# First DFT stage of batches 1 to 7 on quarters of the PE array, four rows at a time

## The chip, the cores and the metric

The kernel runs on one core of one Trainium2 chip. The metric is the device time of one execution in microseconds (us); lower is better. Three runs of the kernel before took 2705.15, 2701.14 and 2705.21 us, median 2705.15.

## The reference

A global filter over the sequence (real FFT along 3008 positions, multiply by a learned complex filter, inverse FFT) and then a feed-forward layer with the activation h - tanh(h), all in float32:

```python
X = np.fft.rfft(x, axis=1)                     # x: 8 x 3008 x 256
Y = X * (filt_r + 1j * filt_i)[None]           # filt: 1505 x 256
y = np.fft.irfft(Y, n=3008, axis=1)
t = y.reshape(24064, 256)
h = t @ w_in                                   # 256 -> 2048
out = (h - np.tanh(h)) @ w_out                 # 2048 -> 256
```

## The kernel before, in words

The transform is done as matmuls. 3008 = 64 x 47, so position n is 47q + r. Sequence rows r and 47 - r are handled together: partitions 0 to 63 of a tile hold the 64 values of q for row r, partitions 64 to 127 those for row 47 - r. So there are 24 such row pairs (r = 0 to 23) for a batch.

- The **first stage** (`first`, L241 to L265) multiplies a row pair by one constant 128x128 matrix `f` (64 + 64 rows in; 4 kinds of 32 frequencies out): one matmul `pf` of 128 rows, 128 columns out and 256 moving columns for each r. XH = 2 values of r make one step: two matmuls into one PSUM bank (L262), a copy by ScalarE to SBUF (`a1`, L263), and a store to a DRAM buffer `ct1` (L264). Each step loads its own piece of `f` (128 KB) and of x. This covers batches 2 to 7 whole and the last two thirds of batch 1: 80 steps. Batch 0 and the rest of batch 1 go through other code in the prologue.
- The **middle stage** (`middle`, L357) reads `ct1` back, goes across the 24 rows (`forth`: matmuls `pa`, `pb`; VectorE forms sums and differences from PSUM, L306 and L307), multiplies by the filter (`filtered`, its last two instructions are L338 and L339), goes back (`back`: matmuls `pe`) and stores `ct2`.
- The **last stage** (`last`, matmuls `pu`) makes 512 tokens at a time (a group; six groups make a batch). Then the feed-forward layer runs over a group in four **units** (u = 0 to 3, 512 of the 2048 hidden columns each): `up` (matmuls `x`, `y`, `z`, L485), `shrink` (the activation: ScalarE L597, L600, L603; VectorE L607), `down` (matmuls `o`, L655). Both products are done by a Strassen-like scheme with seven products, whose operand sums are made on GpSimd (L465 to L468). The first four units (U = 0 to 3) use plain products (`up_plain` L555, `down_plain` L709) while the weights are still converted from float64.

There are 192 units, U = 0 to 191; batch p's feed-forward is units 24p to 24p + 23. The order on every engine is written out by hand. Inside a unit there are five places, `t(0)` to `t(4)`, at which one step of another stage is put in. For a unit U of 4 or above, outside batch 0, TensorE's order is: X product 1, Y product 2, `t(0)`, four `o` matmuls, `t(1)`, X6, Z5, four `o`, `t(2)`, X7, four `o`, X4, `t(3)`, two `o`, `t(4)`, Z3. VectorE empties Y by L508 (after `t(0)`'s instructions in its own order), X by L533, Z by L525 and L541. `planned(p)` spreads the steps of the first stage of batch p + 2 and of the middle stage of batch p + 1 evenly over batch p's units and sorts them by due position. Batch 2's first stage, with what is left of batch 1, lies closer, in units 0 to 6.

PSUM has eight banks: `x`, `y`, `z` for `up`, `o0` to `o3` for `down`, and one, `t`, for the steps put in. `zd` (L1138) gives a step bank `t`, or at some places bank `y` where the step before it holds `t`: at `t(3)` bank `y` if `t(2)` didn't use it; at `t(4)` and `t(0)` always `t`.

In the prologue, `tiled` (L900) keeps TensorE busy until x has landed. It does so with matmuls on a constant tile in four forms: whole array, quarters (up to 64 rows in, 64 columns out), halves (up to 64 rows, 128 columns), whole array.

Of the kernel before, what the change touches and what calls it, by code (L numbers as in the profile page):

```python
# [9 lines left out]
F32 = mybir.dt.float32  # L10
# [5 lines left out]
ALU = mybir.AluOpType  # L16
# [9 lines left out]
XH = 2  # L26
# [21 lines left out]
def _consts():  # L48
# [9 lines left out]
    f = np.zeros((2, NQ, NH, 4, NA))  # L58
    g = np.zeros((4, NA, NH, 2, NQ))
    for r in range(NH):  # L60
        for half, n in ((0, r), (1, NR - r)):
# [4 lines left out]
            f[half, :, r, 0, :-1], f[half, :, r, 1, :-1] = c, -s  # L66
            f[half, :, r, 2, :-1], f[half, :, r, 3, :-1] = -odd * s, odd * c
            plus, minus = (1 + sign(n)) / 2, (1 - sign(n)) / 2
            f[half, :, r, 0, -1], f[half, :, r, 2, -1] = plus, minus
            f[half, :, r, 1, -1], f[half, :, r, 3, -1] = odd * plus, odd * minus  # L70
# [3 lines left out]
            g[1, -1, r, half], g[3, -1, r, half] = odd * plus, odd * minus  # L74
# [18 lines left out]
    f = f[:, :, :, ORDER, :]  # L93
    return [np.ascontiguousarray(v, dtype=np.float32)
            for v in (f.reshape(128, -1), f[:, :, :, 0:2].reshape(128, -1), g.reshape(128, -1), mats, np.eye(128))]

@with_exitstack
def kernel(
# [11 lines left out]
    f_d, half_d, g_d, mats_d, one_d = (nc.inline_tensor(v, name=n).ap()  # L110
                               for v, n in zip(_consts(), ("f", "f_half", "g", "mats", "one")))
# [6 lines left out]

    filt_d = nc.dram_tensor("filt", (len(SLOTS) * KM, 4, DM), F32, kind="Internal")
# [109 lines left out]
    def load_x(t, b, r, n):  # L229
# [3 lines left out]
        if r == 0:  # L233
            nc.sync.dma_start(t[64:128, 0, :], dram(x.tensor, b * SEQ * DM,
                                                    [[NR * DM, 64], [1, DM]]))
        lo = 1 if r == 0 else 0
        nc.sync.dma_start(t[64:128, lo:n, :], dram(x.tensor, (b * SEQ + NR - r - lo) * DM,
                                                   [[NR * DM, 64], [-DM, n - lo], [1, DM]]))
        return t

    def first(b, z, also=()):  # L241
# [3 lines left out]
        def begin(k):  # L245
            b, c = jobs[k]
            w = XH * 128
            f = tr.tile([128, XH, 128], F32, tag="f", bufs=3, name="f")
            nc.sync.dma_start(f, f_d[:, w * c:w * (c + 1)])
            return load_x(tr.tile([128, XH, DM], F32, tag="x", bufs=3, name="x_sb"),  # L250
# [4 lines left out]
        for k, (b, c) in enumerate(jobs):  # L255
            if k + 2 < len(jobs):
                began.append(begin(k + 2))
            xt, f = began.pop(0)
            pf = z("pf", [128, XH, DM])
            a1 = tr.tile([128, XH, DM], F32, tag="a1", bufs=2, name="a1")  # L260
            for i in range(XH):
                nc.tensor.matmul(pf[:, i], f[:, i], xt[:, i], start=True, stop=True)  # L262
            ACT.copy(a1, pf)  # L263
            ACT.dma_start(dram(ct1[b], XH * c * DM, [[NH * DM, 128], [1, XH * DM]]), a1)  # L264
            yield  # L265
# [145 lines left out]
    def turned_rows():  # L411

        for v, src in enumerate((filt_r.tensor, filt_i.tensor)):
            G.dma_start(dram(filt_d, (turned * 4 + 2 + v) * DM,
                             [[DM // 2, 2], [4 * DM, NH], [1, DM // 2]]),
                        dram(src, SEQ // 2 * DM,
                             [[DM // 2, 2], [-NQ * DM, NH], [1, DM // 2]]))
# [430 lines left out]
    psums = []  # L848

    def z1(name, shape):  # L850
        return psums[-1](name, shape)

    with tc.tile_pool(name="tr", bufs=2) as tr, tc.manual_schedule():
# [12 lines left out]
        with tc.tile_pool(name="pro", bufs=1) as pro, \  # L866
# [32 lines left out]

            def tiled():  # L900

                t = filt[2][:, 0]
                banks = [z0("warm", [128, 256]) for _ in range(4)]

                def mm(rows, cols, bank):
                    nc.tensor.matmul(bank[cols], t[rows, 0:cols.stop - cols.start],
                                     t[rows], start=True, stop=True)

                half = slice(0, 64), slice(64, KM)
                out = slice(0, 64), slice(64, 128)  # L910
                for _ in range(6):
                    mm(slice(0, KM), slice(0, 128), banks[0])
                for n in range(4):
                    for i, rows in enumerate(half):
                        for cols in out:
                            mm(rows, cols, banks[2 * (n % 2) + i])
# [398 lines left out]
```

## Time and profile before

| | |
|---|---|
| runs | 2705.15, 2701.14, 2705.21 us |
| profiled execution: time, span | 2702.15 us, 2700.3 us |
| granted TensorE clock over the span | 0.998 |
| TensorE busy | 2670.9 us, 99% |
| ScalarE, VectorE, GpSimd busy | 1722.8, 1651.3, 1289.9 us |
| first stage (L262): matmul instructions, busy | 320, 82.2 us |

A row of a view names the line of the kernel, the engine, the operation, what it writes and reads, how many, and microseconds. PE is TensorE's matmul, PEld its weight load, DVE VectorE, ACT ScalarE, POOL GpSimd, SP the queue that issues most DMAs. A float32 matmul shows as two instructions, so "x4" is two matmuls. The shape "128*128 128x256" is rows in * columns out of the array, then rows x moving columns.

### The profile page before, as it was taken

The page shows a single profiled execution, that of the slowest core. Times are in us where ns is not written, and L with a number is a line of the kernel's source. Part 1 is how long each engine was busy: PE and PEld are TensorE (multiplying, and loading weights), DVE is VectorE, ACT ScalarE, POOL GpSimd, SP SyncE. Part 2 cuts the span into 40 slices and gives each one's busy share as a digit, 9 for nine tenths or more (in the row PEclk, how much of TensorE's full clock was granted, in tenths as well). Part 3 has the DMA queues.
Part 4 walks back from the last instruction along what each step waited for, and adds up shares of the span by engine and source line. Part 5 has one row for each costly group of instructions (what it writes and reads, how often), then busy time and mean ns, then how long its engine had stood idle before and what let it go on. Part 6 is the DMA issues. An engine that isn't in the chain of part 4 may idle for free.

```text
span 2700.3 us, 36549 instructions
## 1 busy us (share of the span) xinstructions
PE 2670.9 (99%) x12950; PEld 2360.7 (87%) x12950; DVE 1651.3 (61%) x2083; ACT 1722.8 (64%) x2595; POOL 1289.9 (48%) x1082
## 2 busy tenths in 40 slices
PE   8999999999999999999999999999999999999998
PEld 7578889988898888988889888898889988898887
DVE  6777766666566664666546665566655666544545
ACT  3566666666666666666666666666666666666665
POOL 4124555454454445545445554455445554554552
PEclk9999999999999999999999999999999999999999
DMA  8754223431242223323233232323322231110110
GB/s 219 233 162 115 56 58 77 107 86 49 63 110 75 80 56 78 98 69 81 54 96 80 68 86 57 92 76 79 88 55 58 52 79 34 31 40 19 24 24 18
DMA packets 341400, 208.09 MB, mean 77 GB/s; under 512 B 227096, under 2 KB 303492, under 8 KB 341144
## 3 DMA queue, kind: packets, MB, share of 16 engines
q1 hardware_dynamic: 298957, 147.45, 22.6%
q10 hardware_dynamic: 38138, 45.63, 5.5%
q0 software_dynamic: 4112, 12.60, 1.7%
q8 instruction: 104, 1.70, 0.3%
q14 instruction: 89, 0.72, 0.1%
HBM read 133.42 MB, written 74.97 MB: 77 GB/s over the span
## 4 chain that ended last, share of the span: by engine, by line
PE 93%; DMA 2%; DVE 2%; ACT 1%; issue 1%; SPq 1%; ACTq 0%; POOL 0%; DVEq 0%
PE o L655 40%; PE x L485 23%; PE z L485 11%; PE y L485 6%; PE pu L447 3%; PE pe L349 3%; PE pf L262 2%; PE pa L301 2%; PE pb L301 1%; PE o L709 1%; DMA gt<-g 0%; DMA mats_sb<-mats 0%; DMA f<-f 0%; ACT y L597 0%; PE o L555 0%
## 5 line engine op out<-in xcount | busy, mean ns | idle before, releaser
L655 PE MATMUL o<-t,wd 128*128 128x256 f32 (+1 forms) x3008 | 759.7, 375 | 0.0
L607 DVE TENSOR_TENSOR h<-h,y 128x1024 f32<-128x1024 f32 (+1 forms) x384 | 513.3, 1337 | 295.7 <-ACT y L603 295.2
L465 POOL TENSOR_TENSOR t<-h 128x512 f32<-128x512 f32 (+1 forms) x186 | 254.1, 1366 | 907.7 <-DVE h L607 836.1
L655 PEld LDWEIGHTS o<-t,wd 128*128 128x128 f32 x3008 | 570.5, 190 | 67.2
L485 PE MATMUL x<-tu,wu 128*128 128x256 f32 (+1 forms) x2256 | 573.0, 376 | 1.6 <-ACT u L491 1.1
L655 PE MATMUL o<-h,wd 128*128 128x256 f32 (+1 forms) x2256 | 570.4, 375 | 1.8 <-DVE h L607 1.8
L485 PEld LDWEIGHTS x<-tu,wu 128*128 128x128 f32 x2256 | 421.5, 190 | 57.5 <-ACT u L491 9.6
L655 PEld LDWEIGHTS o<-h,wd 128*128 128x128 f32 x2256 | 424.2, 190 | 50.3 <-DVE h L607 2.6
L491 ACT COPY s<-x 128x512 f32<-128x512 f32 (+1 forms) x188 | 108.6, 578 | 501.9 <-PE x L485 483.8
L597 ACT ACTIVATE y<-h 128x1024 f32<-128x1024 f32 (+1 forms) x384 | 400.2, 1042 | 13.3 <-ACT a L263 5.2
L600 ACT ACTIVATE y<-y 128x1024 f32<-128x1024 f32 (+1 forms) x384 | 399.2, 1039 | 12.1
L603 ACT ACTIVATE y<-y 128x1024 f32<-128x1024 f32 (+1 forms) x384 | 399.9, 1041 | 7.8 <-DMA x_sb<-in_x_dram 2.7
L525 DVE TENSOR_TENSOR h<-z,u 128x512 f32<-128x512 f32 (+1 forms) x188 | 127.5, 678 | 243.8 <-ACT u L491 243.1
L468 POOL TENSOR_TENSOR t<-h,t 128x512 f32<-128x512 f32 (+1 forms) x186 | 264.3, 1421 | 0.0
L491 ACT COPY u<-x 128x512 f32<-128x512 f32 (+1 forms) x376 | 214.5, 571 | 76.9 <-PE x L485 50.5
L467 POOL TENSOR_TENSOR t<-h 128x512 f32<-128x512 f32 (+1 forms) x186 | 262.9, 1413 | 0.0
L466 POOL TENSOR_TENSOR t<-h,t 128x512 f32<-128x512 f32 (+1 forms) x186 | 255.9, 1376 | 14.6
L533 DVE COPY h<-x 128x512 f32<-128x512 f32 (+1 forms) x188 | 127.9, 680 | 152.8 <-PE x L485 152.2
L485 PE MATMUL x<-ut,wu 128*128 128x256 f32 (+1 forms) x752 | 190.2, 375 | 0.0
L485 PE MATMUL y<-ut,wu 128*128 128x256 f32 (+1 forms) x752 | 190.1, 375 | 0.0
L485 PE MATMUL z<-ut,wu 128*128 128x256 f32 (+1 forms) x752 | 190.1, 375 | 0.0
L485 PE MATMUL z<-tu,wu 128*128 128x256 f32 (+1 forms) x752 | 190.0, 375 | 0.0
(153 smaller groups left out, 3037.4 us busy)
## 6 DMA issues: line engine op xcount, KB each, us to landing
e<-ct SPq DMA_DIRECT2D x47, 512.0 KB
ct<-a ACTq DMA_DIRECT2D x82, 256.0 KB
ct<-e ACTq DMA_DIRECT2D x86, 240.0 KB
a<-ct SPq DMA_DIRECT2D x42, 480.0 KB
ft<-filt SPq DMA_DIRECT2D x42, 480.0 KB
out_dram<-ot SPq DMA_DIRECT2D x1248, 16.0 KB
x_sb<-in_x_dram SPq DMA_DIRECT2D x154, 128.0 KB
gt<-g SPq DMA_DIRECT2D x48, 256.0 KB
```

Of the source, the lines that this page charges most:

```text
L465: by.tensor_sub(t[0], b[0][1], b[0][0])
L466: by.tensor_sub(t[1], b[1][1], t[0])
L467: by.tensor_sub(t[2], b[1][1], b[0][1])
L468: by.tensor_sub(t[3], b[1][0], t[1])
L485: nc.tensor.matmul(bank[:, k], wu[:, q - 1, (2 * u + k) * 128:(2 * u + k + 1) * 128], rhs[q - 1], start=(first and k == 0), stop=True, ski ...
L491: ACT.copy(t, X)
L533: V.tensor_copy(h[:, 2, :, 0:w], X)
L597: ACT.activation(y[k], ht[k], AF.Arctan, scale=TURN)
L600: ACT.activation(y[k], y[k], AF.Tanh, scale=BEND)
L603: ACT.activation(y[k], y[k], AF.Square, scale=SCALE, accum_out=y_sums[:, 2 * U + k // 2:2 * U + k // 2 + 1])
L607: V.tensor_mul(ht[k], ht[k], y[k])
L655: nc.tensor.matmul(product(q), wd[:, q - 1, (2 * u + k) * 128: (2 * u + k + 1) * 128], rhs[q - 1][:, k], start=(u == 0 and k == 0 and q == ...
```

## The change

XH goes from 2 to 4, so a step of the first stage (a **visit** here) now takes four values of r, and there are 40 visits instead of 80. The two halves of a tile's rows are no longer contracted together. A row pair's matrix is now 128x64: 64 columns (cosines; sines with the sign of the half) for each half of the rows. Each visit issues eight matmuls of 64 rows in, 64 columns out and 256 moving columns, in two sets of four that address the four quarters of the array. The upper half of the rows goes to bank `t`, the lower half to bank `y`; two values of r lie on the two halves of the output partitions. ScalarE copies bank `y` to SBUF (`other`), and VectorE then forms sum and difference of bank `t` and that copy into `a1`. The two stores of a visit are put on a list and issued by ScalarE's queue at the next `t`.

Both banks are held by a visit, so it may not stand at `t(0)` of a unit from U = 4 on, where Y is in use; there a due step of the middle stage is taken first. By the order that the program now gives, the visits of batches 3 to 7 stand, counted from the first unit of a batch, at unit 0 `t(1)`, unit 3 `t(4)`, unit 7 `t(3)`, unit 10 `t(3)`, unit 14 `t(1)`, unit 17 `t(3)`, the same in each batch. The ten visits of batch 1's rest and batch 2 stand in units 0 to 6.

`x` and `f` have two buffers instead of three (twice as large for x, the same for f), and the loads for the visit after the next are issued behind a visit's matmuls instead of ahead of them. `a1` has one buffer instead of two.

Since the lower half's sine columns come with the other sign, the fourth kind of the last frequency changes sign: the constants `g` follow, and in the prologue (`turned_rows`) 24 rows of the filter are loaded, negated by VectorE, stored to DRAM and copied from there into the filter buffer, on GpSimd's queue. The prologue's `tiled` gives way to 15 whole-array matmuls (`warmer(15)`), and three small VectorE instructions that built the other columns of batch 0's matrix become one.

```diff
-XH = 2
+XH = 4
...
         for k, (b, c) in enumerate(jobs):
+            xt, f = began.pop(0)
+            banks = z("pf", [128, 2, DM])
+            for n in range(2):
+                for bank, half in zip(banks, rows):
+                    for m, out_half in enumerate(rows):
+                        nc.tensor.matmul(bank[out_half, n], f[half, 2 * m + n], xt[half, 2 * m + n],
+                                         start=True, stop=True)
             if k + 2 < len(jobs):
                 began.append(begin(k + 2))
-            xt, f = began.pop(0)
-            pf = z("pf", [128, XH, DM])
-            a1 = tr.tile([128, XH, DM], F32, tag="a1", bufs=2, name="a1")
-            for i in range(XH):
-                nc.tensor.matmul(pf[:, i], f[:, i], xt[:, i], start=True, stop=True)
-            ACT.copy(a1, pf)
-            ACT.dma_start(dram(ct1[b], XH * c * DM, [[NH * DM, 128], [1, XH * DM]]), a1)
+            a1 = tr.tile([128, 2, 2, DM], F32, tag="a1", bufs=1, name="a1")
+            other = tr.tile([128, 2, DM], F32, tag="e1", bufs=2, name="other")
+            ACT.copy(other, banks[1])
+            V.tensor_add(a1[:, 0], banks[0], other)
+            V.tensor_sub(a1[:, 1], banks[0], other)
+            for m, part in enumerate(rows):
+                written.append((dram(ct1[b], (XH * c + 2 * m) * DM,
+                                     [[NH * DM, 64], [64 * NH * DM, 2], [1, 2 * DM]]),
+                                a1[part].rearrange("p v n c -> p v (n c)")))
...
+        G.dma_start(t, dram(filt_i.tensor, (SEQ // 2 - NQ * (NH - 1)) * DM,
+                            [[NQ * DM, NH], [1, DM]]))
+        turned_to(0, filt_r.tensor, SEQ // 2)
+        yield
+        V.tensor_scalar(out=t, in0=t, scalar1=-1.0, scalar2=None, op0=ALU.mult)
+        G.dma_start(dram(less_d, 0, [[DM, NH], [1, DM]]), t)
+        turned_to(1, less_d, NH - 1)
...
-            tiled()
+            warmer(15, filt[2][:, 0])
...
+            def zd2(name, shape):
+                U, k = now
+                taken[k] = "both"
+                return [ps.tile(shape, F32, tag=tag, bufs=1, name=name) for tag in "ty"]
...
                 def t(k):
                     now[:] = U, k
+                    while written:
+                        ACT.dma_start(*written.pop(0))
...
-                    elif steps and steps[0][0] <= pos:
-                        _, gens, b, what, n = steps.pop(0)
+                    else:
+                        due = [s for s in steps[0:2] if s[0] <= pos and
+                               (k or U < 4 or s[3] is middle)]
+                        if due:
+                            steps.remove(due[0])
```

More of the change, by code (lines that the diff above doesn't have):

```diff
@@ L117 @@
            for b in range(BATCH)]
+    less_d = nc.dram_tensor("less", (NH, DM), F32, kind="Internal")
     filt_d = nc.dram_tensor("filt", (len(SLOTS) * KM, 4, DM), F32, kind="Internal")
@@ L898, in warmer @@
                     nc.tensor.matmul(warm, t[:, 0:128], t, start=True, stop=True)
[L900 to L916, printed above, removed]
-                for n in range(4):
-                    for i, rows in enumerate(half):
-                        mm(rows, slice(0, 128), banks[2 * (n % 2) + i])
-                for _ in range(2):
-                    mm(slice(0, KM), slice(0, 128), banks[0])
             def across(g):
@@ L1120 @@
             rest(SG * (last_g - 1), NA - SG * (last_g - 1), [nc.sync])
-            fs = first(2, z1, [(1, c) for c in range(4, NX)])
+            fs = first(2, z2, [(1, c) for c in range(2, NX)])
             next(fs)
```

75 lines of the change are left out of this document (40 added, 35 removed).

## The prediction

> **What bounds the kernel now.** I read the page's busy shares and its chain of waits first, then the stretches, then the groups of instructions by shape.
>
> ```profile
> span 2700.3 us, 36549 instructions
> PE 2670.9 (99%) x12950; PEld 2360.7 (87%) x12950; DVE 1651.3 (61%) x2083; ACT 1722.8 (64%) x2595; POOL 1289.9 (48%) x1082
> PE 93%; DMA 2%; DVE 2%; ACT 1%; issue 1%; SPq 1%; ACTq 0%; POOL 0%; DVEq 0%
> ```
>
> ```profile
> 420.00:2660.00 2240.00, 2239.67 (x10917) 2006.56 (x10916) 1341.65 (x1631) 1457.17 (x2189) 1115.50 (x916) 1.00 0.26 67
> ```
>
> The second fence gives, from 420 to 2660 us, the length, then busy time of PE, PEld, DVE, ACT and POOL, the granted clock (1.00), the DMA share and GB/s. TensorE is idle for 0.33 us of 2240. So there is no hidden room on it: a matmul less is its full time less, and a wait that TensorE meets is its full time more, since nothing behind can catch up. The other engines have a third of their time free on average, which says nothing about whether they are free at the moment when TensorE needs a bank.
>
> **What the change takes off TensorE.** The groups by shape give the size of the stage, ScalarE's copy and VectorE's kind of operation from PSUM:
>
> ```profile
> L262 PE MATMUL pf<-x_sb,f 128*128 128x256 f32 x320 | 82.2, 379 | 1.9 <-DMA f<-f 1.9
> L263 ACT COPY a<-pf 128x512 f32<-128x512 f32 x80 | 46.6, 582 | 83.7 <-PE pf L262 81.6 <-DMA ct<-a 2.0
> L306 DVE TENSOR_TENSOR xy<-pb,xy 120x512 f32<-120x512 f32 x48 | 33.0, 688 | 23.2 <-PE pb L301 23.2
> ```
>
> A step of two matmuls occupies TensorE from its start to the next start, in the timeline of unit 34:
>
> ```profile
> 567.39 1.03 PE L262 MATMUL pf<-x_sb,f 128*128 128x256 f32 x4
> 567.59 0.69 DVE L533 COPY h<-x 128x512 f32<-128x512 f32 x1 [0.82 <-PE x L485]
> 568.25 1.03 PE L655 MATMUL o<-t,wd 128*128 128x256 f32 x4
> 568.46 0.59 ACT L263 COPY a<-pf 128x512 f32<-128x512 f32 x1 [1.82 <-PE pf L262]
> 569.12 1.03 PE L301 MATMUL pa<-a,mats_sb 120*120 120x256 f32 x4
> ```
>
> 568.25 - 567.39 = 0.86 us, 0.43 a matmul; four values of r cost 1.72. What quarters cost, the prologue's `tiled` shows: 16 quarter matmuls (32 instructions), then 8 halves, then two whole ones.
>
> ```profile
> L906 PE MATMUL warm<-filt 64*64 64x256 f32 x16 | 1.9, 382 | 0.0
> L906 PE MATMUL warm<-filt 56*64 56x256 f32 x16 | 1.9, 382 | 0.0
> ```
>
> ```profile
> 1.45:6.35 4.90, 4.90 (x12) 3.73 (x13) 1.00 0.93 235
> 6.35:8.24 1.89, 1.89 (x34) 1.12 (x33) 1.00 1.05 270
> 10.16:11.13 0.97, 0.97 (x6) 0.68 (x4) 1.00 1.05 283
> ```
>
> Both groups, upper and lower rows, fill the same 1.9 us, so four quarters run side by side: four sets of four in 1.89 us, against 4 x 0.43 = 1.72 for four whole matmuls. The 0.17 over is the way in and out of the form; the two whole matmuls after a change of form take 0.97 instead of 0.86, another 0.11; and the first quarter itself comes late by something that no row separates, which I put at 0.08, between nothing and the 0.11 of the other end. A visit is then two sets, 0.86, and 0.36 for the change of form: 1.22. Against 1.72 that is 0.50 less, and 40 visits give **-20.0**. The ends: form changes free, 40 x 0.86 = -34.4; no gain from the quarters, only the 0.36, +14.4.
>
> The Trainium skill ("TensorEngine Tiling (Array Packing)", Key Properties) states that a change of the tiling mode drains the TensorE. The same page's Theoretical Speedup, up to 2x for each dimension of at most 64, would by itself put -34.4 here. The trace agrees with the drain, by its 0.17 and 0.11.
>
> **What it adds: three waits in every batch.** A visit now ends by ScalarE's copy of bank `y` (0.59), then two VectorE operations on bank `t` (0.69 each); only after the second is `t` free. In unit 34 a visit stands at `t(3)`, and `pa` at `t(4)` writes `t`; only two `o` matmuls lie between. Before, that visit took `y` and `pa` was not held up. From 567.39: the last quarter result is there at about 568.55 (0.08 late, 0.86 of pitch, and some 0.2 for the last instruction's end and the way in), the copy ends at 569.2, sum and difference at 570.6. VectorE's own copy of X (L533) is over by 568.28 and does not matter. TensorE has done visit and `o` at 567.39 + 1.22 + 0.86 = 569.47. It waits 1.1, and picks up with the 0.1 that it also lost after a drain above: **1.2**. Unit 41 has the same with `pe`:
>
> ```profile
> 667.02 1.03 PE L262 MATMUL pf<-x_sb,f 128*128 128x256 f32 x4
> 667.88 1.03 PE L655 MATMUL o<-t,wd 128*128 128x256 f32 x4
> 668.75 0.81 PE L349 MATMUL pe<-xy,mats_sb 120*120 120x256 f32 x3
> ```
>
> `t` free at 667.02 + 3.2 = 670.2, TensorE there at 669.1: **1.2** again. ScalarE queues the visit's two stores behind the same difference at `t(4)`, and behind them stands the copy of that `pa` or `pe`, which is later still; it loses nothing.
>
> The third is unit 38, `t(1)`. The visit needs `y` emptied by L508, and in the new order VectorE does L306 and L307 for the `pb` that now stands at `t(0)` ahead of L508 (before, `pb` stood at `t(1)`):
>
> ```profile
> 613.95 1.71 DVE L338 TENSOR_TENSOR xy<-nn 120x512 f32<-120x512 f32 x1
> 614.27 1.03 PE L485 MATMUL y<-ut,wu 128*128 128x256 f32 x4
> 615.13 1.03 PE L262 MATMUL pf<-x_sb,f 128*128 128x256 f32 x4
> 615.58 1.75 DVE L339 TENSOR_TENSOR xy<-nn 120x512 f32<-120x512 f32 x1
> 616.00 1.89 PE L655 MATMUL o<-h,wd 128*128 128x256 f32 x8
> 617.26 0.68 DVE L541 TENSOR_TENSOR h<-z,u 128x512 f32<-128x512 f32 x1
> 617.72 1.03 PE L301 MATMUL pb<-a,mats_sb 120*120 120x256 f32 x4
> 617.86 0.68 DVE L508 TENSOR_TENSOR h<-y,s 128x512 f32<-128x512 f32 x1
> ```
>
> VectorE is late here already: L338 and L339 take 1.71 and 1.75, and L541 ends at 617.94. With 2 x 0.69 for `pb` put in, L508 runs from 619.3 to 620.0. TensorE has Y from 614.27, then `pb` and four `o` matmuls as the old order has `pf` and `o`: it comes to the visit at 617.72. It waits 2.3, of which the way into quarters hides 0.1: **2.2**. Bounds: nearly none, if L338 and L339 took 0.69 as L306 does (2.1 less), and 4.3, if the two for `pb` took 1.75 as L339 does; I stay with 0.69 for them, the row of the same operation.
>
> The visits at the other three places find room: at unit 31 four pairs of matmuls (3.4) lie before `t` is needed, against 2.0 for copy, sum and difference; at unit 27 two pairs (1.7) before Y needs bank `y`, against 0.6; at unit 24 `pa` takes `y`, and six matmuls lie between. I take nothing for them, at most 0.2 each.
>
> The five batches 3 to 7 have the same places: 5 x (1.2 + 1.2 + 2.2) = **+23.0**, against 5 x 6 x 0.50 = 15 of the gain. The Trainium skill (the same page, Performance Considerations, PSUM Bottleneck) says that tiling speeds up TensorE but not the emptying of PSUM, which may then bind; these three waits are that in this kernel, and no row of before shows it happen.
>
> **Batch 2's ten visits, in units 0 to 6.** There VectorE also converts the weights:
>
> ```profile
> 112.80:141.60 28.80, 28.80 (x105) 18.39 (x104) 27.55 (x57) 21.85 (x35) 2.02 (x3) 1.00 0.75 233
> ```
>
> ```profile
> 128.51 1.09 DVE L607 TENSOR_TENSOR h<-h,y 128x896 f32<-128x896 f32 x1
> 129.74 1.67 PE L709 MATMUL o<-h,wd 128*128 128x448 f32 x4
> ```
>
> VectorE is busy for 27.55 of 28.80 us, and a product starts 0.14 us after the L607 that it needs (129.60 to 129.74). About four visits fall here; each puts 1.38 us on VectorE and up to 0.6 in which it waits, in order, for ScalarE's copy: 5.5 to 8 us that has to come out of TensorE's time but for the small leads. I take **+6** for the ten visits, between 0 (the leads were enough) and 12 (the other visits there cost as much). The 1.9 us that L262 waited for `f` (its row above) lie here too, and the ten visits load 1.3 MB of `f` instead of 2.6: **-1.9**, at worst 0.
>
> **The prologue.** Fifteen whole matmuls take 4.9 us for the first six (the 1.45:6.35 row) and 9 x 0.43 = 3.9, 8.8 instead of 9.7: -0.9 if x is there by then, else 0. On GpSimd's queue the negated rows go out after the stores at 40.21 and the copy from them waits for their landing, ahead of the addition that feeds the product at 48.06:
>
> ```profile
> 40.21 1.52 POOL L976 DMA_DIRECT2D ct<-e  x2
> 48.06 0.59 PE L972 MATMUL pe<-nn,mats_sb 120*120 120x256 f32 x2
> 55.59 0.69 PE L972 MATMUL pe<-nn,mats_sb 120*120 120x256 f32 x2 [1.26 <-POOL nn L327]
> ```
>
> ```profile
> ct<-e POOLq DMA_DIRECT2D x10, 240.0 KB, 3.9
> filt<-in_filt_r_dram POOLq DMA_DIRECT2D x1, 24.0 KB, 7.3
> ```
>
> 41.7 plus 0.7 for the issue, 3.9 to 7.3 to land, 0.7 for the next issue and 1.3 for the addition is 48.3 to 51.7: 0.2 to 3.6 late, of which the 1.26 that TensorE waits at 55.59 anyway swallows a part. Together -0.9 to +2.4; I take **0**.
>
> Edits at nothing: SP now waits for a visit before it issues the loads of the one after next; behind that stand stores of results of the places that follow, and three or four whole units lie between visits of batches 3 to 7, so no load is late. ScalarE makes 40 copies fewer (23 us), off the path. VectorE has 80 operations more, 55 us of its 1050 free.
>
> **The sum.** On the profiled execution's own time, 2702.15: -20.0 + 23.0 + 6 - 1.9 + 0 = +7.1, 2709.3. That execution lies between the runs shown (2701.14 to 2705.21) and 1.7 below their mean, so a median of new runs should come to **2711**, 0.2% above the median of before. About 0.2%, 5.4 us, is what a measurement of this kernel can tell from no change, so this stands at the edge.
>
> **Rivals.** *The change of form is hidden* (a visit costs 0.86): 40 x 0.36 = 14.4 less, 2697, faster. Against: the 1.89 and 0.97 rows. 0.12. The Trainium skill ("TensorEngine Tiling (Array Packing)", Theoretical Speedup) gives this case, since its factors count no switch.
> *VectorE is not late at unit 38*, the rival for faster by one wait: if L338 and L339 run at 0.69, because GpSimd's L465 to L468 no longer fall on them, L508 is done when TensorE arrives, and 5 x 2.2 go: 2700. It decides as soon as VectorE gains 2.2 of the 3.46 us that the two take. Against: neither engine's order there changes. 0.15, of which 0.10 is below 2699.7.
> *VectorE bounds units 0 to 6*: the ten visits cost 12 or more, GpSimd's wait in the prologue its 2.4: 2719 and up to 2728. For it: the 27.55 of 28.80. 0.17.
> *Quarters overlap only when they read the same columns*: in `tiled` both column halves streamed the same tile, here they stream different r. Each set of four would take 0.86: 40 x 0.86 more, 2745. No row speaks against it, but the trace issues four separate streams already. 0.06.
>
> **How the numbers follow.** The forecast holds 0.50, with a range of its own of 2703 to 2720: 0.32 slower, 0.18 within 0.2%. The rivals hold 0.12, 0.15, 0.17 and 0.06. Faster 0.12 + 0.10 = 0.22; same 0.18 + 0.05 = 0.23; slower 0.32 + 0.17 + 0.06 = 0.55. The range 2694 to 2727 leaves out the last rival and the outer parts of the first and third.
>
> **What would show it.** Right: L262 with 640 instructions in about 45 us; waits of TensorE for VectorE of 1.2 us before `pa` in unit 34 and `pe` in unit 41 and 2.2 before the visit in unit 38, alike in five batches; some 6 us of idle TensorE between 100 and 180 us. Wrong: no wait at those three places, or visits of 0.9 or of 2 us between the starts around them.

## The result, and the profile after

| | before | after |
|---|---|---|
| median (range) | 2704.58 us (2701.14 to 2705.21) | 2716.88 us (2715.20 to 2720.79) |
| profiled execution: time, span | 2702.15, 2700.3 us | 2716.88, 2715.0 us |

The changed kernel takes 1.0052 times as long (95% interval 1.0040 to 1.0063). The medians differ by 12.3 us and the ratio stands for 14; the time lies in the upper half of the predicted range of 2694 to 2727.

From the page of the changed kernel: span, busy times and the chain of waits. Line numbers are those of the changed kernel; L504 is `up` (before L485), L674 `down`, L311 `pa` and `pb`, L359 `pe`, L466 `pu`, L728 the plain `down`.

```profile
span 2715.0 us, 36862 instructions
PE 2661.3 (98%) x13236; PEld 2327.6 (86%) x13236; DVE 1698.7 (63%) x2158; ACT 1699.5 (63%) x2555; POOL 1291.0 (48%) x1084
PE 92%; DVE 4%; ACT 1%; DMA 1%; issue 1%; SPq 0%; POOL 0%; ACTq 0%; DVEq 0%; POOLq 0%
```

TensorE has 10 us less to do and is idle for 24 us more (2715.0 - 2661.3 = 53.7, before 29.4). VectorE's share of the chain rose from 2% to 4%. VectorE is still busy for only 63% on average: the average says nothing of the places where it is late.

The groups of instructions of a visit, shapes apart:

```profile
L262 PE MATMUL pf<-x_sb,f 64*64 64x256 f32 x640 | 47.1, 390 | 8.6 <-DVE xy L317 6.6 <-issue 2.0
L268 ACT COPY other<-pf 128x512 f32<-128x512 f32 x40 | 23.2, 581 | 56.3 <-PE pf L262 56.3
L269 DVE TENSOR_TENSOR a<-pf,other 128x512 f32<-128x512 f32 x40 | 27.6, 690 | 53.4 <-ACT other L268 49.0 <-DMA ct<-a 4.4
L270 DVE TENSOR_TENSOR a<-pf,other 128x512 f32<-128x512 f32 x40 | 27.2, 680 | 0.0
```

The quarters do overlap: 640 instructions take 47.1 us, where the 320 of the kernel before took 82.2. But the last column is new: TensorE stood 8.6 us before visits (1.9 before), and VectorE once stood 4.4 us for a store out of `a1`.

Where in time the 14.7 us went is read from the start of each unit's first X product, after less before (first profiles of both):

| unit | 0 | 6 | 9 | 12 | 24 | 48 | 72 | 96 | 120 | 144 | 191 |
|---|---|---|---|---|---|---|---|---|---|---|---|
| us later | 1.0 | 6.6 | 6.9 | 11.0 | 11.0 | 12.3 | 13.5 | 14.8 | 16.0 | 16.2 | 16.2 |

Units 0 to 12 cost 10.1 us, batches 3 to 6 1.24 us each, batch 7 0.23, and the end behind the last unit is 1.5 us shorter, which nothing here explains. So batches 3 to 7, from which most of the predicted loss came, cost little; the ten early visits cost most.

A visit and a wait in the timeline, unit 34 (`t(3)`, then `pa` at `t(4)`):

```profile
576.77 1.10 PE L262 MATMUL pf<-x_sb,f 64*64 64x256 f32 x16
577.80 1.13 PE L674 MATMUL o<-t,wd 128*128 128x256 f32 x4
577.96 0.58 ACT L268 COPY other<-pf 128x512 f32<-128x512 f32 x1 [2.04 <-PE pf L262]
578.58 0.69 DVE L269 TENSOR_TENSOR a<-pf,other 128x512 f32<-128x512 f32 x1 [1.00 <-ACT other L268]
579.19 0.68 DVE L270 TENSOR_TENSOR a<-pf,other 128x512 f32<-128x512 f32 x1
579.97 1.10 PE L311 MATMUL pa<-a,mats_sb 120*120 120x256 f32 x4 [1.04 <-issue]
```

The visit lasts 577.80 - 576.77 = 1.03 to the next start. The start before it and the first pitch behind it are 0.10 longer than the normal 0.215 each, so it costs 1.22 to 1.23. `pa` starts at 579.97, 2.17 after the `o` products' start, which last 0.86 and 0.10 for the form: 1.2 of waiting, and 0.10 after the end of L270 (579.87). Bank `t` was awaited (stores_behind, below, shows it).

Unit 38, where the visit at `t(1)` waits for bank `y`:

```profile
623.82 1.71 DVE L348 TENSOR_TENSOR xy<-nn 120x512 f32<-120x512 f32 x1
625.46 1.76 DVE L349 TENSOR_TENSOR xy<-nn 120x512 f32<-120x512 f32 x1
627.14 0.68 DVE L560 TENSOR_TENSOR h<-z,u 128x512 f32<-128x512 f32 x1
627.74 0.68 DVE L316 TENSOR_TENSOR xy<-pb,xy 120x512 f32<-120x512 f32 x1
628.45 0.69 DVE L317 TENSOR_TENSOR xy<-pb,xy 120x512 f32<-120x512 f32 x1
629.06 0.68 DVE L527 TENSOR_TENSOR h<-y,s 128x512 f32<-128x512 f32 x1
629.29 1.59 PE L262 MATMUL pf<-x_sb,f 64*64 64x256 f32 x16 [1.53 <-DVE xy L317]
630.80 0.92 PE L504 MATMUL x<-tu,wu 128*128 128x256 f32 x3
```

The order is the predicted one: the filter's last two operations of 1.7 us, L560, the two for `pb`, and only then L527, which frees Y. The visit waits in two steps: its upper quarters start behind L317, which frees `t`, its lower ones at 629.79, 0.05 behind L527; it takes 1.51 instead of 1.02. So it waits for both of its banks in turn, and the prediction had named `y` alone. With the 1.6 of idle time ahead of it (1.53 in the row and the rest of the `o` product's pitch) that is 2.1 us. The list of waits for batches 3 to 7 has these three places five times each and nothing else:

```profile
PE pf L262 <- DVE xy L317: 6.6, 5, 1.5
PE pe L359 <- DVE a L270: 5.4, 5, 1.1
PE pa L311 <- issue: 5.2, 5, 1.0
```

The early part, units 0 to 12: TensorE's waits from 88 to 260 us, then stretches (length, then busy PE, PEld, DVE, ACT, POOL, granted clock, DMA share, GB/s).

```profile
PE x L504 <- ACT u L510: 4.7, 3, 2.8
PE x L504 <- DVE h L552: 4.3, 2, 2.9
PE pf L262 <- issue: 2.0, 1, 2.0
PE pu L466 <- DVE a L270: 1.9, 1, 1.9
```

```profile
100.00:141.60 41.60, 37.67 (x178) 19.56 (x178) 38.64 (x73) 26.67 (x44) 3.43 (x5) 1.00 0.78 214
174.50:177.50 3.00, 3.00 (x10) 2.35 (x9) 2.97 (x5) 1.93 (x3) 2.08 (x2) 0.53 0.68 175
229.30:232.00 2.70, 2.68 (x6) 2.18 (x7) 1.15 (x3) 2.67 (x5) 0.00 (x0) 0.50 0.65 163
```

VectorE is busy for 38.64 of 41.60 us, and TensorE, which has the most to do in this kernel, for only 37.67. Behind the two longest waits the granted clock is half for 3.4 us (174.69 to 178.10 and 229.30 to 232.71), which costs 1.5 us each time. Two rows show what held the engines there:

```profile
172.09 0.69 DVE L269 TENSOR_TENSOR a<-pf,other 128x512 f32<-128x512 f32 x1 [4.44 <-DMA ct<-a]
224.93 0.37 ACTq L364 DMA_DIRECT2D ct<-e  x1
225.35 1.06 ACT L616 ACTIVATE y<-h 128x1024 f32<-128x1024 f32 x1 [3.41 <-DMA out_dram<-ot]
```

At 172 VectorE waits 4.44 us until the store of the visit before has left the one buffer `a1`; the copy of X and so TensorE's next X product stand behind it. At 225 ScalarE, with `pe`'s copy done at 221.93, cannot issue the store of it until an earlier store of results has landed; its next activation is 3.41 us late, and TensorE waits 2.8 us for a copy that ScalarE does later.

### The profile page after: what moved, and what is told of

It reads as the page before. It is cut to its first block, busy times and chain, and to the rows that moved or that the text cites. A ratio compares the mean times of both kernels' runs of the same rounds, so it can differ in the third digit from the quotient of the medians.

```text
span 2715.0 us, 36862 instructions
## 1 busy us (share of the span) xinstructions
PE 2661.3 (98%) x13236; PEld 2327.6 (86%) x13236; DVE 1698.7 (63%) x2158; ACT 1699.5 (63%) x2555; POOL 1291.0 (48%) x1084
## 4 chain that ended last, share of the span: by engine, by line
PE 92%; DVE 4%; ACT 1%; DMA 1%; issue 1%; SPq 0%; POOL 0%; ACTq 0%; DVEq 0%; POOLq 0%
PE o L674 40%; PE x L504 23%; PE z L504 11%; PE y L504 6%; PE pu L466 3%; PE pe L359 3%; PE pa L311 2%; PE pb L311 1%; PE pf L262 1%; DVE h L626 1%; PE pf L910 0%; PE warm L920 0%; DVE xy L349 0%; DVE a L270 0%; DMA ct<-a 0%
## 5 line engine op out<-in xcount | busy, mean ns | idle before, releaser
L674 PE MATMUL o<-t,wd 128*128 128x256 f32 (+1 forms) x3008 | 762.4, 376 | 0.0
L484 POOL TENSOR_TENSOR t<-h 128x512 f32<-128x512 f32 (+1 forms) x186 | 256.4, 1379 | 936.2 <-DVE h L626 858.5
L626 DVE TENSOR_TENSOR h<-h,y 128x1024 f32<-128x1024 f32 (+1 forms) x384 | 520.3, 1355 | 284.8 <-ACT y L622 284.2
L674 PEld LDWEIGHTS o<-t,wd 128*128 128x128 f32 x3008 | 571.2, 191 | 71.4 <-issue 5.8
L504 PE MATMUL x<-tu,wu 128*128 128x256 f32 (+1 forms) x2256 | 574.9, 377 | 4.8 <-ACT u L510 4.8
L674 PE MATMUL o<-h,wd 128*128 128x256 f32 (+1 forms) x2256 | 571.4, 376 | 1.7 <-DVE h L626 1.7
L504 PEld LDWEIGHTS x<-tu,wu 128*128 128x128 f32 x2256 | 422.2, 191 | 62.0 <-ACT u L510 10.5
L674 PEld LDWEIGHTS o<-h,wd 128*128 128x128 f32 x2256 | 425.4, 191 | 50.0 <-DVE h L626 2.6
L487 POOL TENSOR_TENSOR t<-h,t 128x512 f32<-128x512 f32 (+1 forms) x186 | 266.9, 1435 | 0.0
L485 POOL TENSOR_TENSOR t<-h,t 128x512 f32<-128x512 f32 (+1 forms) x186 | 259.6, 1396 | 14.6
L486 POOL TENSOR_TENSOR t<-h 128x512 f32<-128x512 f32 (+1 forms) x186 | 254.5, 1368 | 0.0
L552 DVE COPY h<-x 128x512 f32<-128x512 f32 (+1 forms) x188 | 127.8, 680 | 148.9 <-PE x L504 148.3
L504 PE MATMUL x<-ut,wu 128*128 128x256 f32 (+1 forms) x752 | 191.0, 377 | 4.4 <-DVE h L552 4.3
L504 PE MATMUL y<-ut,wu 128*128 128x256 f32 (+1 forms) x752 | 191.0, 377 | 0.0
L504 PE MATMUL z<-ut,wu 128*128 128x256 f32 (+1 forms) x752 | 190.8, 376 | 0.0
L504 PE MATMUL z<-tu,wu 128*128 128x256 f32 (+1 forms) x752 | 190.4, 376 | 0.0
```

What stands on the lines that cost most here:

```text
L484: by.tensor_sub(t[0], b[0][1], b[0][0])
L485: by.tensor_sub(t[1], b[1][1], t[0])
L486: by.tensor_sub(t[2], b[1][1], b[0][1])
L487: by.tensor_sub(t[3], b[1][0], t[1])
L504: nc.tensor.matmul(bank[:, k], wu[:, q - 1, (2 * u + k) * 128:(2 * u + k + 1) * 128], rhs[q - 1], start=(first and k == 0), stop=True, ski ...
L552: V.tensor_copy(h[:, 2, :, 0:w], X)
```

## The experiments

All edits are to the changed kernel (except one run of the kernel before), and "later" is always against the first profile of before. Ratios are against the kernel before on the same chip.

**y_after_visit**

```diff
                               k == 3 and taken.get(2) != "y" or
+                              k == 4 and taken.get(3) == "both") else "t"
```

> What comes at t(4) right behind a visit at t(3) takes bank y, which ScalarE's copy frees, instead of bank t, which is free only after the difference. Theory A (TensorE waits there for VectorE's sum and difference): both waits of every batch go, 5 x (1.20 + 1.25) = 12.3 us, 2716.9 becomes 2704.6, and no other wait grows. Theory B (ScalarE's copy of bank y is as late as the difference, because ScalarE's chain is in front of it): the waits stay under another name, and at most 4 us go: 2713 or more.

Measured: 2712.41 against 2701.62, ratio 1.0038 (1.0024 to 1.0051). The waits for L270 went, but half of the gain came back: batches 3 to 7 are 6.6 us shorter than in the changed kernel, not 12.3. TensorE's new waits from 430 to 2010 us, then ScalarE and TensorE in unit 34 and 35:

```profile
PE y L504 <- ACT e L362: 1.8, 5, 0.4
PE y L504 <- ACT xy L314: 1.6, 5, 0.3
```

```profile
582.16 1.28 ACTq L1249 DMA_DIRECT2D ct<-a  x2
583.48 0.59 ACT L314 COPY xy<-pa 120x512 f32<-120x512 f32 x1 [2.67 <-DVE h L626]
584.12 1.13 PE L504 MATMUL y<-ut,wu 128*128 128x256 f32 x4 [0.31 <-ACT xy L314]
```

`pa` is there at 582.1, but its copy stands in ScalarE's queue behind the two issues of the visit's stores, which wait for the difference and take 1.28. It frees bank `y` 1.4 us late, and Y of the next unit waits. Theory A has the bank right, theory B that a wait stays under another name; neither had the stores.

**later_visit**

```diff
-                               (k or U < 4 or s[3] is middle)]
+                               (k or U < 4 or s[3] is middle) and
+                               (s[3] is middle or k != 1 or
+                                (taken.get("unit"), taken.get(0)) != (U, "pb"))]
```

> No visit stands at t(1) when pb has just taken bank t at t(0): the visit of unit 38 moves to t(2), the filter step to t(3). Theory A (VectorE reaches y's addition late because of its order there: the two products of 1.7 us and pb's sum and difference come first): the wait of 1.69 and the 0.42 inside the visit go, 4 x 2.10 and 1.07 in batch 7, 9.5 us: 2707.4. Theory B (VectorE is late in unit 38 anyway, whatever stands where): the wait turns up before the next matmul that needs a bank from VectorE, and at most 4 us go: 2713 or more.

Measured: 2712.32 against 2701.62, ratio 1.0039 (1.0026 to 1.0053). The wait before the visit is gone. A new one stands before `pu` in unit 39 and in its like of three more batches (0.13, 0.80, 0.15 and 0.40 us), again behind the stores: in unit 39 they are issued from 638.40 on for 4.02 us, and `e`'s copy, which frees the bank for `pu`, comes at 642.52. Batches 3 to 7 cost 0.4 us less than before in all, instead of 5.2 more: 5.6 won of the 9.5 that theory A expected. VectorE's order is what made unit 38 late, but not all of the wait is won by moving the visit.

**spread_visits**

```diff
-                f = [spread(*((NX + 4, 4, LEAD) if b == 2 else (NX, 0.2, LAG)), firsts, b, first)
+                f = [spread(4, 4, 24, firsts, b, first) + spread(NX, LEAD, LAG, firsts, b, first)
+                     if b == 2 else spread(NX, 0.2, LAG, firsts, b, first)
```

> Of the ten visits of units 0 to 6 only batch 1's four stay (units 0 to 3, one in each); batch 2's six go to units 6 to 18, where VectorE has room. Theory A (in units 0 to 6 VectorE's work and the one buffer a1, held by the store of the visit before, make TensorE wait): of the waits of 2.06, 1.75, 1.56, 3.11 and of the half clock behind the longest (1.6) some 7 go, less 1.2 for a new wait at unit 16, where pb stands behind a visit: 2711. Theory B (visits cost the same wherever they stand, since the copies of filters on the DMA queues, not VectorE, hold them): within 2 us of 2716.9. The wait of 2.99 at unit 9 for ScalarE's held store, with its half clock, is expected to move or go, as the DMAs in front of it change their places: up to 4.6 more.

Measured: 2721.66 against 2701.62, ratio 1.0069 (1.0055 to 1.0083), a miss. The visit of unit 2 now stands at `t(4)`, right ahead of `pu` in unit 3:

```profile
PE pu L466 <- issue: 7.5, 1, 7.5
```

`pu` needs bank `t`, and its sum and difference (126.46 to 127.74) stood in VectorE's queue behind 8 us of other work, most of it the conversion of weights (the visit had ended at 118.6). Behind this wait the granted clock was 0.50 from 122.85 to 133.09, and in two of the batches 3 to 7 it halved behind unit 38. Fewer visits, but one at a worse place: it speaks for VectorE's queue, against theory B, and does not size it.

**light_sums**

```diff
-            V.tensor_add(a1[:, 0], banks[0], other)
-            V.tensor_sub(a1[:, 1], banks[0], other)
+            V.tensor_add(a1[:, 0, :, 0:w], banks[0][:, :, 0:w], other[:, :, 0:w])
+            V.tensor_sub(a1[:, 1, :, 0:w], banks[0][:, :, 0:w], other[:, :, 0:w])
```

> The ten visits of units 0 to 6 form sum and difference of 8 columns of 256 only, in one standing buffer (batches 1 and 2 get zeros elsewhere); matmuls, copy and stores stay. Theory A1 (VectorE's 10 x 1.38 us of work is what is too much there): the waits of 2.06, 1.75, 1.56 shrink to a third and the one of 3.11 goes, with its half clock: some 8 us, 2709. Theory A2 (the buffer a1, in which VectorE has to wait for the landing of the store before, is what holds): the 3.11 and its half clock stay, at most 4 us go: 2713. Theory B (neither): within 1.5 us of 2716.9.

The kernel leaves out most of the sums: in the ten early visits it forms 8 of every 256 columns, and what it stores of batches 1 and 2 is zero elsewhere.

Measured: 2712.87 against 2701.62, ratio 1.0041 (1.0027 to 1.0055). TensorE's waits from 88 to 260 us, then VectorE in unit 5:

```profile
PE x L512 <- ACT u L518: 2.7, 3, 2.2
PE x L512 <- DVE h L560: 2.5, 2, 1.5
```

```profile
168.80 0.17 DVE L277 TENSOR_TENSOR a<-pf,other 128x16 f32<-128x16 f32 x1 [5.07 <-DMA ct<-a]
168.97 0.68 DVE L560 COPY h<-x 128x512 f32<-128x512 f32 x1
```

From unit 0 to unit 12 the lag grows by 0.3 us instead of 10.1: theory A1 for the most part. Of the 9.7 won, 2.3 lie at unit 9, where ScalarE's hold cost 2.2 us and brought no half clock this time. The whole time shows less, since this profile starts unit 0 later by 2.8 (1.0 in the changed kernel's), and batch 7 had a stretch of half clock. L560 here is the copy of X that is L552 in the changed kernel, eight lines further down. VectorE still waits in front of it for the store out of `a1`, 5.07 us against 4.44, with next to no sums to do. So theory A2 holds for this place: TensorE's wait shrank from 2.9 to 1.5 us and lost its half clock, but did not go. In all 5.8 us of TensorE's waits between unit 0 and 12 are left of 12.9.

**early_whole.** The ten early visits become twenty steps in the old form (two whole matmuls on bank `t` or `y`, one copy, one store), from a 128-column matrix.

```diff
+    def first_whole(b, z, also=()):
...
-            fs = first(2, z2, [(1, c) for c in range(2, NX)])
+            fs = first_whole(2, z1, [(1, c) for c in range(2, NX)])
...
-                f = [spread(*((NX + 4, 4, LEAD) if b == 2 else (NX, 0.2, LAG)), firsts, b, first)
+                f = [spread(*((2 * NX + 8, 4, LEAD) if b == 2 else (NX, 0.2, LAG)), firsts, b, first)
```

> The ten visits of units 0 to 6 are made as the kernel before makes them: twenty steps of two whole matmuls, one copy by ScalarE, no sum and difference. Batches 3 to 7 keep the quarters. Theory A (units 0 to 6 lose 10 us because VectorE, full with the weights, must give banks free): TensorE's lag behind the kernel before goes from 11.0 us at unit 24 to about 1, and to 6 at the end, 5 x 1.24: 6 us above before instead of 14. Theory B (the delay there comes from the loads in blocks of four r with two buffers instead of three, which stay): at unit 24 some 6 us or more remain, and 10 us or more at the end.

Measured: 2709.07 against 2703.06, ratio 1.0026 (1.0017 to 1.0035). The lag is 0.1 at unit 24 instead of 11.0, with the loads in blocks of four r and two buffers kept: theory A. (From unit 0 to 24 that is 2.2 us less than in the first profile of before, and 0.2 more than in its second one, before_again.) At the end it is 8.6 instead of 6, because two of the five batches cost 2.9 instead of 1.24. Both have half clock behind the same wait of unit 38; below, that batch, and the same stretch of the changed kernel:

```profile
950.00:953.30 3.30, 3.30 (x9) 2.59 (x8) 3.00 (x5) 2.13 (x4) 0.00 (x0) 0.50 0.00 0
960.00:963.50 3.50, 3.50 (x22) 2.77 (x17) 2.22 (x3) 2.34 (x4) 0.00 (x1) 1.00 0.01 2
```

**two_copies**

The early visits (`also`) keep the old lines.

```diff
-            ACT.copy(other, banks[1])
-            V.tensor_add(a1[:, 0], banks[0], other)
-            V.tensor_sub(a1[:, 1], banks[0], other)
+            if also:
...
+            else:
+                ACT.copy(a1[:, 0], banks[0])
+                ACT.copy(other, banks[1])
+                V.tensor_sub(a1[:, 1], a1[:, 0], other)
+                V.tensor_add(a1[:, 0], a1[:, 0], other)
```

> In batches 3 to 7 ScalarE copies both banks of a visit, and VectorE forms difference and sum from SBUF; units 0 to 6 as they are. Theory A (bank t is late because VectorE empties it): the waits before pa in unit 34 and pe in unit 41 go, 5 x 2.45 = 12 us, also without the bank's change of y_after_visit; unit 38 stays. From 14 us above before to about 2. Theory B (ScalarE has no room for a second copy of 0.6 us there): its copies come behind its chain of activations of 1.06 us, and new waits of about 0.5 us at the six visits take half of it back: 7 or 8 above before.

Measured: 2718.13 against 2703.06, ratio 1.0053 (1.0039 to 1.0067): nothing won. The waits for L270 are gone, but a new one stands once a batch, in unit 29 of batch 3 and its like:

```profile
PE x L510 <- ACT u L516: 6.7, 5, 1.5
```

```profile
815.16 1.51 DVE L276 TENSOR_TENSOR a<-a,other 128x512 f32<-128x512 f32 x1
816.70 1.49 ACTq L1254 DMA_DIRECT2D ct<-a  x2
818.24 0.95 ACT L622 ACTIVATE y<-h 128x896 f32<-128x896 f32 x1 [2.73 <-issue]
```

Out of SBUF the second operation takes 1.51 us here (0.68 out of PSUM). ScalarE holds the issue of the stores until the second has ended, and its chain of activations is 2.73 us late (that the slow sums are the reason is argued here; best_parts, which keeps two copies at one place only, has no such wait). Theory B named the right engine, but not its reason: its room is enough, its queue is held.

**stores_behind.** y_after_visit's edit, and:

```diff
-                    while written:
-                        ACT.dma_start(*written.pop(0))
+                    behind = written[:]
+                    written.clear()
...
+                    for w in behind:
+                        ACT.dma_start(*w)
                     converting(2)
```

> As y_after_visit, and the two stores of a visit are issued behind the step that follows, not ahead of it. Theory A (the new wait of 0.5 us before y in units 35 and 42 comes from ScalarE, which issues the stores, 1.3 us, ahead of the copy that frees bank y): these waits go, and the whole 12 us of units 34 and 41 are won, against the 5 us of y_after_visit: 2 us above before. Theory B (the copy is late for ScalarE's own chain): as y_after_visit, 10 above before.

Measured: 2708.28 against 2703.06, ratio 1.0020 (1.0011 to 1.0029). ScalarE in unit 34, the copy now ahead of the stores:

```profile
575.93 0.59 ACT L314 COPY xy<-pa 120x512 f32<-120x512 f32 x1 [1.31 <-PE pa L311]
575.99 1.28 ACTq L1273 DMA_DIRECT2D ct<-a  x2
```

Of the waits from 430 to 2010 us only the one before the visit of unit 38 is left, with the same 6.6 us. Batches 3 to 7 cost 4.4 us less than before, against 5.2 more: 9.6 of the 12.3, with two stretches of half clock (1.6 each) that the changed kernel's profile lacks. Theory A.

**all_parts.** early_whole, two_copies, later_visit and the stores behind the step.

> early_whole, two_copies, later_visit and the stores behind the step together. If the account is whole, each of the batches 3 to 7 now gives its 6 x 0.50 = 3.0 us, with nothing lost but a few tenths: 15 us, less 1 for units 0 to 6: 14 below before, ratio 0.995. If VectorE is late in unit 38 all the same, some 1.3 us a batch are left: 8 below before.

Measured: 2692.94 against 2703.06, ratio 0.9966 (0.9952 to 0.9980). Unit 38 has no wait left; the one of two_copies in unit 29 and its like is there in all five batches, 9.0 us together, so the time came between the two that were expected.

**best_parts.** early_whole, stores_behind and later_visit, and the two copies only for the visit that later_visit moves:

```diff
-            ACT.copy(other, banks[1])
...
+            if now[1] != 2:
+                ACT.copy(other, banks[1])
+                V.tensor_add(a1[:, 0], banks[0], other)
+                V.tensor_sub(a1[:, 1], banks[0], other)
+            else:
+                ACT.copy(a1[:, 0], banks[0])
...
```

> Units 0 to 6 with whole matmuls (early_whole), bank y behind a visit and the stores behind the step (stores_behind), the visit of unit 38 at t(2) (later_visit), and two copies by ScalarE for that visit alone. Theory A (with banks t and y given free in time a visit is worth its 0.50 us of TensorE, and the new wait of 1.5 us in unit 29 of two_copies comes from the sums out of SBUF, behind which ScalarE issues the stores): each of the batches 3 to 7 gives 3.0 us, 15 in all, less 1 for units 0 to 6: 14 below before, 0.995. Theory B (that wait comes from somewhere else, or unit 38 finds a new one): 1.5 us a batch are left, 7 below before, as all_parts.

Measured: 2683.49 against 2702.82, ratio 0.9930 (0.9917 to 0.9944): 19 us faster than the kernel before. The page's span and busy times, and the stretch from 440 to 2640 us:

```profile
span 2681.6 us, 36719 instructions
PE 2656.5 (99%) x13156; PEld 2334.9 (87%) x13156; DVE 1687.3 (63%) x2138; ACT 1706.9 (64%) x2570; POOL 1300.9 (49%) x1084
440.00:2640.00 2200.00, 2200.00 (x11034) 1955.88 (x11034) 1366.27 (x1675) 1426.69 (x2142) 1115.78 (x910) 1.00 0.26 64
```

TensorE does not stand still once in 2200 us. The five batches give 3.4 us each, 16.9 in all, against 15 expected: besides 1.22 for 1.72, an old step could lengthen what followed it a little (in unit 36, which lost its step, the stretch from the first `o` product to the last `pe` took 9.50 us instead of 9.68 without the step; the other units were not taken apart). Theory A.

**late_loads.** The first call of `first`'s generator moves behind `last(0, z1)`.

> As the changed kernel, but the first two visits' loads of f and x, 512 KB of x instead of 256 before the change, are issued behind the loads of e for the first unit, not ahead. Theory A (these loads share the DMA engines with the rows that the first pu waits for): TensorE's wait before the first pu, 2.5 us in the changed kernel's profile and 1.7 before, falls to 1.7 or less, and unit 0 starts a microsecond earlier; the first visit may wait for x instead, up to 2 us. Theory B (the wait is for the round trip of the rows themselves): it stays at 2.5 us or more. The whole time moves by no more than 2 us either way.

**before_again.** The kernel before, unchanged.

> The kernel before, unchanged, for a second profile of it. If the wait before the first pu (1.7 us in its first profile) belongs to the kernel, it is 1.5 to 2 us again, and TensorE's units start within 0.3 us of where they did; if it varies by the chip, as in the changed kernels (2.5 to 4.6), it may be 3 or more, and the prologue is then no part of the difference.

Measured: late_loads 2720.31 against 2702.82, ratio 1.0069 (1.0054 to 1.0085); before_again one run of 2700.70. The first `pu` of late_loads, of the changed kernel and of before_again (here its first 14 of 16 instructions), with the wait before it:

```profile
86.12 3.46 PE L466 MATMUL pu<-gt,e 128*128 128x128 f32 x16 [3.25 <-DMA ct<-a]
```

```profile
85.33 3.09 PE L466 MATMUL pu<-gt,e 128*128 128x128 f32 x16 [2.31 <-DMA f<-f]
```

```profile
86.43 1.80 PE L447 MATMUL pu<-gt,e 128*128 128x128 f32 x14 [3.19 <-DMA f<-f]
```

The wait is 3.2 us with the visits' loads moved away and 3.2 in the kernel before itself (1.55 in its first profile, 2.31 in the changed kernel's): it stays, as theory B had it, and is no property of the change. What follows it is. From the start of the first `pu` to unit 0 the kernel before took 1.81 us in both of its profiles, at full clock; the changed kernel took 2.88, at a granted clock of 0.50 from 85.94 to 89.35, and in all twelve profiles with the changed prologue it was 2.88 to 3.44. That unit 0 starts 0.99 later in before_again and 0.96 in the changed kernel is therefore a coincidence: the one waited longer, the other ran slower. The prologue can be 1.1 to 1.6 us of the difference; with two profiles of the old one, chance is not ruled out. late_loads came out slower still, by more than the 2 us that were expected at most: its profile has half clock behind unit 38 in three of five batches, at 1.65 us each.

before_again shows one thing more: the 1.9 us of its first profile in which L262 waited for `f` are not there. Its units 0 to 4 take 2.1 us less, so measured from unit 0 on against this profile, the changed kernel loses 12.5 us by unit 12, not 10.1.

**rows_by_sync**

```diff
-            before = done, back(b, g, xy, z)
+            before = done, back(b, g, xy, z, (nc.sync, nc.sync))
```

> As the changed kernel, but the rows that pe gives (the stores of e into ct2 by L364) are issued on SyncE's queue, not on ScalarE's. Theory A (at unit 9 ScalarE is held because the issue of such a store waits for the landing of an earlier store of results, and TensorE's 2.99 us and the half clock of 1.6 behind it come from that): the wait at unit 9 goes, the lag behind before from unit 9 to unit 12 falls from 4.1 to under 1 us, and the whole time by 3 to 5 us. Theory B (TensorE is held there by something that the ten visits leave late, whatever queue issues that store): 2 us or more of wait stay between units 9 and 10.

Measured: 2715.85 against 2703.30, ratio 1.0054 (1.0037 to 1.0071). ScalarE at unit 9:

```profile
222.29 0.59 ACT L362 COPY e<-pe 120x512 f32<-120x512 f32 x1 [1.14 <-PE pe L359]
222.77 1.06 ACT L616 ACTIVATE y<-h 128x1024 f32<-128x1024 f32 x1
```

The activation follows the copy at once. The lag from unit 9 to 12 falls from +4.1 to -0.6: theory A for the place. The whole time does not show the 4 us: the profiled run took 2711.02, the others up to 2719.41, and this spread is larger than what is sought.

## Why the prediction was right, and where its sum was not

The sum gave 2709.3 for the profiled execution, and it took 2716.88. The sign, the range and the mechanism hold; the terms are off in both directions. Units 0 to 24 cost 11.0 us more than summed and batches 3 to 7 2.8 less; unit 0 starts 1.0 later and the end is 1.5 shorter. That the miss is 7.6 and not 11 is luck, for the errors have different causes.

- **The visit.** Predicted 1.22, measured 1.22 to 1.23. The rival *change of form hidden* (0.86) is refuted by the 1.03 between starts, the rival of serial quarters by the 47.1 us.
- **The three waits.** Predicted 1.2, 1.2 and 2.2 in each batch, measured 1.20, 1.25 and 2.1. That bank `t` is what `pa` and `pe` wait for is shown by stores_behind, which removes both with another bank; that unit 38 is late by the order there is shown by later_visit. The rival *VectorE is not late at unit 38* is refuted: the last two operations of the filter took 1.71 and 1.76, as before. In batch 7 unit 38 waited 1.1 only, which is not explained. Batches 3 to 7 came to +5.2 against +8.0 (23.0 - 15): 1.0 from batch 7, some 2 from the visits' 3.4 instead of 3.0 a batch.
- **"ScalarE loses nothing" by the stores at `t(4)`** was true of the changed kernel, where the copy behind them waits anyway. As soon as the bank is free earlier, they cost TensorE 0.1 to 1.5 us at a place (later_visit, y_after_visit, two_copies).
- **The ten early visits: the step that failed by its size.** From unit 0 to 24 the sum had -5.0 + 6 - 1.9 = -0.9; measured +10.1. That they are the cause is shown by early_whole, which brings the lag at unit 24 from 11.0 to 0.1; that VectorE's sums in them are the main part is shown by light_sums, which brings its growth from 10.1 to 0.3 and yet keeps 5.8 of 12.9 us of waits. Of the 11.0 missed, the waits for VectorE or for banks behind it (2.06, 1.97, 1.56, 3.11 and 0.62, less 1.12 that before had, and 1.5 of half clock) make 9.7 against 6: +3.7. The wait of 1.9 for `f` was no property of the kernel before (before_again has none), so there was nothing to win; the changed kernel has one of 2.2 near there, which the end of L270 at 106.90 puts down to bank `t` (the visit starts at 107.00): +2.1. ScalarE's hold at unit 9, 3.0 and 1.6 of half clock, was in no part of the prediction: +4.6; rows_by_sync takes it away. The last 0.6 is not placed.
- **What it had not seen**: that `a1` with one buffer ties VectorE to the landing of a store (4.4 us, and 5.1 in light_sums), and that a wait can halve the clock behind it.
- **The prologue**, taken at 0, is open between 0 and 1.6: the wait before the first `pu` is in before_again too, the half clock behind it is not. The wait on GpSimd's queue that the rival added did not come: the product `pe` at the prologue's end starts at 74.16, against 75.03 and 74.38 before.

*VectorE bounds units 0 to 6* (2719 to 2728) was the nearest rival: the early visits' waits for VectorE cost 9.7, between the 6 taken and its 12; with ScalarE's hold, which early_whole nearly takes away too, they come to 14.3. What stays open: why the store of results that held ScalarE at unit 9 landed late in the changed kernel (4.1 us after its issue at 220.82), while in the kernels whose early steps are whole the place costs TensorE 0.5 us or less; what decides whether a wait halves the clock when TensorE was busy for about half of the time around it; and what of the 1.1 to 1.6 us behind the prologue is chance.

## What to carry to other kernels

When a step is made faster on the bounding engine, follow each of its banks to the instruction that frees it, and look at what stands ahead of it in its engine's queue; a copy by an engine with room frees a bank sooner than arithmetic on a crowded one, as long as nothing that waits stands ahead of it in its queue (stores_behind). Put DMA issues behind the copies that free banks, for an issue that waits holds its engine. Average use says little: the visits cost some 1.0 us each in units 0 to 12, where VectorE was full, and gained some 0.5 each in batches 3 to 7 of best_parts, where banks came free in time. And take two profiles of the kernel before: a wait that only one of them has is no gain to count on.

## What the runs showed of the hardware

- The way into quarters of the array and out again costs 0.36 us for two sets of four (1.22 against 2 x 0.43); inside, four quarters with four different streams run at the pace of one whole matmul.
- After pauses of 1.5 to 7.5 us the granted clock was 0.50 for 3.41, 6.83 or 10.24 us (changed kernel: 85.94 to 89.35, 174.69 to 178.10, 229.30 to 232.71; spread_visits: 122.85 to 133.09), beginning up to 2 us after the pause. In each of the 14 traces all changes of the clock lie whole multiples of 3.41 us apart. So what counts is how a pause falls on this grid. Of the steps of the grid at full clock, from 80 us to 25 us before the last matmul's end, all 22 in which TensorE was busy for under 40% were followed by half clock, 17 of the 56 with 40 to 60%, and none of the others. The 1.53 us of idle time in unit 38 leave 55% at the least, and brought it in two of five batches of early_whole, three of five of late_loads, none of the changed kernel.
- The Trainium skill ("TensorE: Matmul & The Clock Gate", What's actually happening) gives the half rate after an idle window of about 3.4 us that runs free; the traces agree with the free window and its length, but a pause of 1.53 us, less than half of it, was enough here.
- VectorE's sum and difference of 128x512 took 0.69 and 0.68 us with an operand in PSUM, and 0.73 and 0.83 on the mean with both in SBUF (two_copies, 30 each), 1.51 at the longest shown here.
